# Row runs for v and q, two queues and a new order for the first loads of a fused linear-attention and two-MLP kernel

## The chip, the cores and the metric

The kernel runs on one core of a Trainium2 chip. The metric is the time of one execution on the device, in microseconds. Five engines work side by side, each through its own list of instructions in order: TensorE (PE in the profile; its weight loads are listed as PEld), VectorE (DVE), ScalarE (ACT), GpSimd (POOL) and SyncE (SP). Matmuls write to PSUM, which VectorE and ScalarE read. Transfers between memory (HBM) and the on-chip SBUF are issued by SP, or by ScalarE, and are carried out by 16 DMA engines.

## The reference

```python
# q, k, v: [batch 8, heads 8, sequence 576, head_dim 64]
q_s = exp(q - max(q, axis=-1));  q_s = q_s / (sum(q_s, axis=-1) + 1e-09)
k_s = exp(k - max(k, axis=2));   k_s = k_s / (sum(k_s, axis=2) + 1e-09)
kv = einsum('bhsd,bhse->bhde', k_s, v)
x = einsum('bhsd,bhde->bhse', q_s, kv)       # then to [4608 tokens, 512]
x2 = relu(x @ w_in)**2 @ w_out               # 512 -> 2048 -> 512
g = x2 @ w_gate
out = (silu(g) * (x2 @ w_val)) @ w_out2      # 512 -> 1536 -> 512
```

Softmax runs over head_dim for q and over the sequence for k. The weights come as 64-bit numbers and are turned into 32-bit ones on the chip.

## The kernel before

The 4608 tokens are cut into 9 blocks of 512. The first part of the program goes through the blocks with attention and the first MLP, the second part (from about 720 us on) does the second MLP, with weight operands that the first part has prepared and stored. Products are made as three single-pass matmuls on a high and a low part of each operand (`mm3`, L110; the parts are made by `split`, a cast on ScalarE and a subtraction on VectorE, L104 and L105).

**Attention.** Heads go in four pairs `hp`. `kv_unit(b, hp)` makes the normalised product of k and v for a batch and a pair: maxima over k's rows on VectorE (L336 to L338), a transpose on TensorE and one more maximum (L341, L343), a broadcast back through TensorE (L346), a subtraction (L347), exp on ScalarE (L353), then 12 products of 96 rows, 6 for each head, of k's 64 columns by 65 columns of v (L358). The 65th column of v is ones, so that the last column of the result is the denominator (L363, L364); ScalarE scales the rest (L367). k and v lie in SBUF with 96 partitions of 6 rows of the sequence each: partition p holds rows 6p to 6p + 5. In k these six rows stand in one run; in v each row of 64 is followed by a one, so a load of v lands in runs of 64 numbers (L294). `q_unit` makes q's softmax: a maximum over each row (L376), 8 exps of 64 columns with the maximum as bias, written over the tile (L380), a sum, a reciprocal and a multiplication (L383 to L386). `q_transpose` (L393) and `x_pair` follow, and give the block of x, transposed, as the right operand of the first MLP.

**First MLP.** For each of 16 slices f, `h_mm` makes the first product (`ph<-xT,w`), `g_of` its squared relu, and `acc_mm` adds the second product to four accumulators (`acc<-g,w`). In block 0 the weights are converted on the way: `w1.step(1)` loads a 64-bit tile, takes it to 32 bits in four steps (ScalarE L138, VectorE L140, L144 and L148, through a PSUM buffer of the pool `ps_a`, which has two and also serves `kv_unit` and `q_transpose`), and splits it (ScalarE L189, GpSimd L191). w1 holds `in` and `out` tiles in the order in which the block uses them.

**Order.** The order of SP's instructions is that of the program text (`manual_schedule`). On the other engines it is set when the program is built, by a planner that takes the instructions by their order in the program and by its own estimate of when each could start; on the chip it is fixed. In the head of the program SP loads, by the list in L722, k, q and v of block 0 into space lent by the weight pool, with the first three weight tiles in between; the plan of L735 then starts the units of the four pairs at ticks 0 to 10. Batch 1 and later ones are worked off inside the MLP's slices, as `attention_plan` says.

Of the kernel before, what the change touches and what calls it, by code (L numbers as in the profile page):

```python
# [8 lines left out]
F32 = mybir.dt.float32  # L9
F32R = mybir.dt.float32r  # L10
I32 = mybir.dt.int32
AF = mybir.ActivationFunctionType
ALU = mybir.AluOpType
AX = mybir.AxisListType
# [3 lines left out]
P = 128  # L18
EPS = 1e-9
# [3 lines left out]
def tile_linear_attention_two_mlps(  # L23
# [29 lines left out]
    nc = tc.nc  # L53
    B, H, S, D = q.shape
# [3 lines left out]
    T = 512  # L58
    TJ = T // P
# [5 lines left out]
    CK = 96  # L65
    NC = S // CK
# [5 lines left out]
    const = ctx.enter_context(tc.tile_pool(name="const", bufs=1))  # L72
# [19 lines left out]
    att = ph0.enter_context(tc.tile_pool(name="att", bufs=1, side="right"))  # L92
    sp = ph0.enter_context(tc.tile_pool(name="sp", bufs=2, side="right"))
# [9 lines left out]
    def split(hi, lo, src, eng=None):  # L103
        nc.scalar.copy(hi, src)  # L104
        (eng or nc.vector).tensor_tensor(lo, src, f32(hi), op=ALU.subtract)  # L105
# [172 lines left out]

    kvs = [att.tile([P, NP, 2, P], F32R, name=f"kv{i}") for i in range(2)]
    kf = att.tile([P, P], F32, name="kf")  # L280
    vt1 = att.tile([CK, 2, NC, D + 1], F32, name="vt")
    kts, qs, qT, xT = {}, {}, {}, {}

    def load_k(b, hp, t=None):
# [2 lines left out]
        nc.sync.dma_start(t, k[b, 2 * hp:2 * hp + 2].rearrange("h (p c) d -> p h c d", c=NC))  # L287
        return t

    def load_v(b, hp, t=None):  # L290
        if t is None:
            t = vt1
        for h in range(2):
            nc.sync.dma_start(  # L294
                t[:, h, :, 0:D], v[b, 2 * hp + h].rearrange("(p c) d -> p c d", c=NC)
            )
        return t

    def load_kv(b, hp):
        kt = vt = None  # L300
        if b == 1 and hp % 2:

            kt, vt = (
                raws.tile([P, T], w_in.dtype, name="wraw", tag="wraw").bitcast(F32) for _ in range(2)
            )
            kt = kt[:CK, 0:2 * NC * D].rearrange("p (h c d) -> p h c d", h=2, c=NC)
            vt = vt[:CK, 0:2 * NC * (D + 1)].rearrange("p (h c d) -> p h c d", h=2, c=NC)
            nc.gpsimd.memset(vt[:, :, :, D:D + 1], 1.0)
        kts[b, hp] = load_k(b, hp, kt), load_v(b, hp, vt)

    def runs(i):
# [8 lines left out]
    def load_q(i, hp, t=None):  # L320
        if t is None:
            t = qp.tile([P, TJ, 2, D], F32, name="qs", tag="qs")
        for p0, n, b, s in runs(i):
            for h in range(2):
                nc.sync.dma_start(
                    t[p0:p0 + n, :, h, :],
                    q[b, 2 * hp + h, s:s + n * TJ, :].rearrange("(p j) d -> p j d", j=TJ),
                )
        qs[i, hp] = t

    def kv_unit(b, hp):

        kt, vt = kts.pop((b, hp))
        m3 = sp.tile([CK, 2, NC // 2, D], F32, name="m3", tag="m3", bufs=1)
        m1 = sp.tile([CK, 2, D], F32, name="m1", tag="m1")
        nc.vector.tensor_tensor(m3, kt[:, :, 0:3], kt[:, :, 3:6], op=ALU.max)  # L336
        nc.vector.tensor_tensor(m1, m3[:, :, 0], m3[:, :, 1], op=ALU.max)
        nc.vector.tensor_tensor(m1, m1, m3[:, :, 2], op=ALU.max)  # L338
        yield
        pt = ps_a.tile([P, T], F32, name="pa", tag="pa")  # L340
        nc.tensor.transpose(pt[:, 0:CK], m1.rearrange("p h d -> p (h d)"), ident[:CK, :CK])  # L341
        mx = col.tile([P, 1], F32, name="mx", tag="mx")
        nc.vector.tensor_reduce(mx, pt[:, 0:CK], axis=AX.X, op=ALU.max)  # L343
        yield
        pb = ps_a.tile([P, T], F32, name="pa", tag="pa")
        nc.tensor.transpose(pb[:CK, 0:P], mx.to_broadcast([P, CK]), ident)  # L346
        nc.vector.tensor_tensor(  # L347
            kt, kt,
            pb[:CK, 0:P].rearrange("p (h d) -> p h d", h=2).unsqueeze(2).to_broadcast([CK, 2, NC, D]),
            op=ALU.subtract,  # L350
        )
        yield
        nc.scalar.activation(kt, kt, AF.Exp)  # L353
        yield
        pk = ps_a.tile([P, T], F32, name="pa", tag="pa")
        for c in range(NC):
            for j in range(2):
                nc.tensor.matmul(  # L358
                    pk[j * D:(j + 1) * D, 0:D + 1], lhsT=kt[:, j, c, :], rhs=vt[:, j, c, :],
                    start=(c == 0), stop=(c == NC - 1),  # L360
                )
        rd = col.tile([P, 1], F32, name="rd", tag="rd", bufs=1)
        nc.vector.tensor_scalar(rd, pk[:, D:D + 1], EPS, None, op0=ALU.add)  # L363
        nc.vector.reciprocal(rd, rd)  # L364
        for j in range(2):
            r = slice(j * D, (j + 1) * D)
            nc.scalar.activation(kf[r, r], pk[r, 0:D], AF.Copy, scale=rd[r])  # L367
        kv = kvs[b % 2]
        split(kv[:, hp, 0], kv[:, hp, 1], kf)
        yield  # L370

    def q_unit(i, hp):

        t = qs.pop((i, hp))
        m = sp.tile([P, TJ, 2], F32, name="qm", tag="qm")
        nc.vector.tensor_reduce(m, t, axis=AX.X, op=ALU.max, negate=True)  # L376
        yield
        for j in range(TJ):
            for h in range(2):
                nc.scalar.activation(t[:, j, h], t[:, j, h], AF.Exp, bias=m[:, j, h:h + 1])  # L380
        yield
        r = sp.tile([P, TJ, 2], F32, name="qr", tag="qr")
        nc.vector.tensor_reduce(r, t, axis=AX.X, op=ALU.add)  # L383
        nc.vector.tensor_scalar(r, r, EPS, None, op0=ALU.add)
        nc.vector.reciprocal(r, r)  # L385
        nc.gpsimd.tensor_tensor(t, t, r.unsqueeze(3).to_broadcast([P, TJ, 2, D]), op=ALU.mult)  # L386
        qs[i, hp] = t
# [318 lines left out]


    with tc.manual_schedule(engines={mybir.EngineType.SP}):
        nc.gpsimd.memset(vt1[:, :, :, D:D + 1], 1.0)
        nc.gpsimd.memset(kf, 0.0)  # L710


        def borrowed():
            return f32(w_slot(wpb)).rearrange("p t n -> p (t n)")

        for hp in range(NP):
            kt = borrowed()[:CK, 0:2 * NC * D].rearrange("p (h c d) -> p h c d", h=2, c=NC)
            vt = borrowed()[:CK, 0:2 * NC * (D + 1)].rearrange("p (h c d) -> p h c d", h=2, c=NC)
            nc.gpsimd.memset(vt[:, :, :, D:D + 1], 1.0)
            qt = borrowed()[:, 0:T].rearrange("p (j h d) -> p j h d", h=2, j=TJ)  # L720
            kts[0, hp], qs[0, hp] = (kt, vt), qt
        for what in "k0 k1 q0 v0 k2 q1 k3 v1 w v2 w q2 q3 w v3".split():  # L722
            if what == "w":
                w1.load()
                continue
            hp = int(what[1])
            if what[0] == "k":
                load_k(0, hp, kts[0, hp][0])
            elif what[0] == "v":
                load_v(0, hp, kts[0, hp][1])  # L730
            else:
                load_q(0, hp, qs[0, hp])

        plan = []
        steps = ((1, 1, 5, 8), (1, 2, 5, 9), (2, 3, 7, 10), (4, 4, 8, 10))  # L735
# [14 lines left out]
        for n in range(NB * NF + LAG):  # L750
            i, f = divmod(n, NF)
# [97 lines left out]
```

## Time and profile before

| | |
|---|---|
| median of 3 runs | 1699.56 us (1696.88 to 1700.6) |
| the profiled execution | 1697.3 us |
| its span, first to last instruction | 1695.2 us |
| TensorE busy in it | 1664.2 us, 98% |
| VectorE, ScalarE, GpSimd busy | 930.4, 865.3, 273.8 us |
| mean granted TensorE clock | 0.998 of full speed |

The profile is of one execution, and its times run from the first instruction of its span. A row names the line of the kernel, the engine, the operation, the written tile and the tiles read. Busy shares of TensorE come from modelled ends of pipelined matmuls, so a busy TensorE need not be at its peak.

### The profile page before, as it was taken

Reading aid. Unit: us, or ns where it says so; the run is one execution under the profiler, and the core shown is the slowest. Engines: PE = TensorE matmul, PEld = TensorE weight load, DVE = VectorE, ACT = ScalarE, POOL = GpSimd, SP = SyncE. Lnnn points to the kernel's source line nnn. Section 1 sums busy time; section 2 is a strip of 40 time slices with the busy share of each in tenths; the row PEclk is TensorE's granted clock in tenths of the full one; section 3 lists DMA queues with packets and bytes.
Section 4 is the critical chain, followed back from the end, with each engine's and each line's share of the span. In section 5 each row is a group of like instructions: output and inputs, shape, how many; then the busy total and the mean of one; then the engine's idle time right before and its main releaser. Section 6 shows DMA issues by size and latency. Waiting matters only on the chain.

```text
span 1695.2 us, 23439 instructions
## 1 busy us (share of the span) xinstructions
PE 1664.2 (98%) x8406; PEld 1377.4 (81%) x8406; DVE 930.4 (55%) x1650; ACT 865.3 (51%) x1701; POOL 273.8 (16%) x260
## 2 busy tenths in 40 slices
PE   5999999999999999999999999999999999999998
PEld 3778888878888887788788888888878888888898
DVE  7884545555554564554242457644765476446646
ACT  6885656555565655665443345333543354335434
POOL 2661101112010111111000211021101210121020
PEclk9999999999999999999999999999999999999999
DMA  9653434443443434332233677867686678666897
GB/s 231 177 165 89 128 108 134 144 115 111 128 128 120 144 124 115 108 131 88 81 100 99 191 217 215 248 196 214 212 244 192 205 214 260 197 199 203 252 387 276
DMA packets 221315, 292.00 MB, mean 172 GB/s; under 512 B 124816, under 2 KB 152464, under 8 KB 221200
## 3 DMA queue, kind: packets, MB, share of 16 engines
q1 hardware_dynamic: 220080, 289.33, 55.6%
q8 instruction: 67, 1.10, 0.3%
q10 hardware_dynamic: 1120, 1.18, 0.2%
q14 instruction: 48, 0.39, 0.1%
HBM read 238.55 MB, written 51.90 MB: 171 GB/s over the span
## 4 chain that ended last, share of the span: by engine, by line
PE 91%; DVE 3%; DMA 2%; ACT 2%; issue 1%; POOL 0%; SPq 0%; DVEq 0%; ACTq 0%; POOLq 0%
PE ps L110 45%; PE ph L110 22%; PE acc L110 21%; PE pa L358 1%; PE pa L393 1%; DMA od<-wst 1%; DMA x<-x2d 1%; DVE wst L105 1%; ACT wst L104 0%; ACT w L380 0%; DMA wraw<-in_moe_w_out_dram 0%; DVE wbits L148 0%; DMA kt<-in_k_dram 0%; DVE pa L144 0%; DVE xT L105 0%
## 5 line engine op out<-in xcount | busy, mean ns | idle before, releaser
L110 PE MATMUL ps<-xo,wu 128*128 128x512 f32 (+1 forms) x2520 | 518.2, 368 | 0.0
L110 PEld LDWEIGHTS ps<-xo,wu 128*128 128x128 f32 x2520 | 439.0, 189 | 78.7
L110 PE MATMUL acc<-g,w 128*128 128x512 f32 x1728 | 433.1, 396 | 4.6 <-ACT g L104 1.8
L110 PE MATMUL ph<-xT,w 128*128 128x512 f32 x1728 | 421.4, 393 | 2.3 <-ACT w L189 1.2
L110 PEld LDWEIGHTS ph<-xT,w 128*128 128x128 f32 x1728 | 321.8, 188 | 72.9 <-ACT w L189 1.6
L110 PEld LDWEIGHTS acc<-g,w 128*128 128x128 f32 x1728 | 316.3, 188 | 76.1 <-DVE g L105 4.1
L110 PE MATMUL ps<-uo,wu 128*128 128x512 f32 (+1 forms) x1260 | 259.9, 368 | 1.3 <-DVE uo L105 1.3
L110 PEld LDWEIGHTS ps<-uo,wu 128*128 128x128 f32 x1260 | 219.3, 189 | 41.2 <-DVE uo L105 2.1
L460 ACT ACTIVATE r<-ph 128x512 f32<-128x512 f32 x144 | 86.3, 599 | 220.6 <-PE ph L110 220.2
L105 DVE TENSOR_TENSOR g<-r,g 128x512 fp32r<-128x512 f32 x128 | 91.5, 715 | 190.4 <-ACT g L104 190.4
L104 ACT CAST uo<-u 128x512 fp32r<-128x512 f32 (+1 forms) x210 | 120.8, 580 | 124.7 <-PE ps L110 53.4
L659 POOL TENSOR_TENSOR u<-u 128x512 f32<-128x512 f32 (+1 forms) x30 | 35.4, 1181 | 761.2 <-DVE u L655 761.2
L105 DVE TENSOR_TENSOR uo<-u,uo 128x512 fp32r<-128x512 f32 (+1 forms) x210 | 131.6, 645 | 47.4 <-ACT uo L104 47.3
L654 DVE TENSOR_TENSOR u<-u,ps 128x512 f32<-128x512 f32 (+1 forms) x60 | 38.0, 634 | 215.9 <-ACT u L653 215.9
L609 ACT COPY ps<-ps 128x512 f32<-128x512 f32 x126 | 72.0, 571 | 136.6 <-PE ps L110 135.4
L461 ACT ACTIVATE r<-r 128x512 f32<-128x512 f32 x144 | 91.2, 633 | 3.0
L104 ACT CAST g<-r 128x512 fp32r<-128x512 f32 x144 | 89.4, 621 | 3.2
L235 POOL TENSOR_TENSOR wsum<-wbits 128x256 f32<-128x256 f32 x36 | 35.3, 990 | 308.4 <-DVE wbits L148 255.0
L380 ACT ACTIVATE qs<-qs,qm 128x64 f32<-128x64 f32 x256 | 69.6, 340 | 21.0 <-DVE qm L376 15.5
L386 POOL TENSOR_TENSOR qs<-qs,qr 128x512 f32<-128x512 f32 x32 | 34.4, 1076 | 250.8 <-DVE qr L385 146.5
L653 ACT ACTIVATE u<-ps 128x512 f32<-128x512 f32 (+1 forms) x60 | 33.4, 556 | 51.6 <-PE ps L110 51.5
L618 ACT COPY p<-ps 128x512 f32<-128x512 f32 x63 | 37.1, 588 | 41.6 <-PE ps L110 40.9
(111 smaller groups left out, 1404.5 us busy)
## 6 DMA issues: line engine op xcount, KB each, us to landing
wu<-gvd SPq DMA_DIRECT2D x210, 512.0 KB, 4.4
wu<-od SPq DMA_DIRECT2D x105, 512.0 KB, 4.4
gvd<-wst SPq DMA_DIRECT2D x84, 256.0 KB, 2.3
od<-wst SPq DMA_DIRECT2D x42, 256.0 KB, 2.2
w<-in_moe_w_in_dram SPq DMA_DIRECT2D x16, 512.0 KB, 6.5
w<-in_moe_w_out_dram SPq DMA_DIRECT2D x16, 512.0 KB, 5.2
x2d<-e SPq DMA_DIRECT2D x32, 256.0 KB, 2.4
x<-x2d SPq DMA_DIRECT2D x32, 256.0 KB, 5.4
```

The lines of the kernel that those rows point to most:

```text
L104: nc.scalar.copy(hi, src)
L105: (eng or nc.vector).tensor_tensor(lo, src, f32(hi), op=ALU.subtract)
L110: nc.tensor.matmul(ps, lhsT=w[s], rhs=x[t], start=start and n == 0, stop=stop and n == 2, skip_group_check=more,)
L235: nc.gpsimd.tensor_tensor(to, x, y, op=op)
L380: nc.scalar.activation(t[:, j, h], t[:, j, h], AF.Exp, bias=m[:, j, h:h + 1])
L386: nc.gpsimd.tensor_tensor(t, t, r.unsqueeze(3).to_broadcast([P, TJ, 2, D]), op=ALU.mult)
L460: nc.scalar.activation(r, ph, AF.Relu)
L461: nc.scalar.activation(r, r, AF.Square)
L609: nc.scalar.copy(x, y)
L618: nc.scalar.copy(x, y)
L654: nc.vector.tensor_tensor(u, u, gate, op=ALU.mult)
L659: nc.gpsimd.tensor_tensor(s1, a21, a22, op=ALU.add)
```

## The change

Four things are changed. v's tiles get another layout: three groups for six rows, each with a one, two rows of 64 in a run, and a one (130 numbers); a load lands in runs of 128 numbers. A product with an even row reads the one ahead of its row and writes columns 0 to 64 of the result, one with an odd row reads the one behind its row and writes columns 1 to 65, so that the denominator is the sum of columns 0 and 65. Two products with a column of zeros come first and write column 65. This holds for all 32 units. q of block 0 is loaded by one DMA for a pair, four rows in a run, into a tile of its own; the exps read it and write the tile in the order used before. The first loads are ordered anew: v of pairs 0 and 1 is issued by ScalarE, all else by SP, and the three weight tiles come after the last q. An exp of one column is put in front of them on ScalarE.

```diff
@@ -278,7 +278,8 @@
 
     kvs = [att.tile([P, NP, 2, P], F32R, name=f"kv{i}") for i in range(2)]
     kf = att.tile([P, P], F32, name="kf")
-    vt1 = att.tile([CK, 2, NC, D + 1], F32, name="vt")
+    vt1 = att.tile([CK, 2, NC // 2, 2 * D + 2], F32, name="vt")
+    zero = const.tile([P, 1], F32, name="zero")
     kts, qs, qT, xT = {}, {}, {}, {}
 
     def load_k(b, hp, t=None):
@@ -287,12 +288,22 @@
         nc.sync.dma_start(t, k[b, 2 * hp:2 * hp + 2].rearrange("h (p c) d -> p h c d", c=NC))
         return t
 
-    def load_v(b, hp, t=None):
+    def v_words(words):
+
+        t = words[:CK, 0:NC * (2 * D + 2)].rearrange("p (h m e) -> p h m e", h=2, m=NC // 2)
+        v_ones(t)
+        return t
+
+    def v_ones(t):
+        nc.gpsimd.memset(t[:, :, :, 0:2 * D + 2:2 * D + 1], 1.0)
+
+    def load_v(b, hp, t=None, by=nc.sync):
         if t is None:
             t = vt1
         for h in range(2):
-            nc.sync.dma_start(
-                t[:, h, :, 0:D], v[b, 2 * hp + h].rearrange("(p c) d -> p c d", c=NC)
+            by.dma_start(
+                t[:, h, :, 1:2 * D + 1],
+                v[b, 2 * hp + h].rearrange("(p m x) d -> p m (x d)", m=NC // 2, x=2),
             )
         return t
 
@@ -304,8 +315,7 @@
                 raws.tile([P, T], w_in.dtype, name="wraw", tag="wraw").bitcast(F32) for _ in range(2)
             )
             kt = kt[:CK, 0:2 * NC * D].rearrange("p (h c d) -> p h c d", h=2, c=NC)
-            vt = vt[:CK, 0:2 * NC * (D + 1)].rearrange("p (h c d) -> p h c d", h=2, c=NC)
-            nc.gpsimd.memset(vt[:, :, :, D:D + 1], 1.0)
+            vt = v_words(vt)
         kts[b, hp] = load_k(b, hp, kt), load_v(b, hp, vt)
 
     def runs(i):
@@ -353,18 +363,25 @@
         nc.scalar.activation(kt, kt, AF.Exp)
         yield
         pk = ps_a.tile([P, T], F32, name="pa", tag="pa")
+        for j in range(2):
+            nc.tensor.matmul(
+                pk[j * D:(j + 1) * D, D + 1:D + 2], lhsT=kt[:, j, 0, :], rhs=zero[:CK],
+                start=True, stop=False, skip_group_check=True,
+            )
         for c in range(NC):
+            m, x = divmod(c, 2)
             for j in range(2):
                 nc.tensor.matmul(
-                    pk[j * D:(j + 1) * D, 0:D + 1], lhsT=kt[:, j, c, :], rhs=vt[:, j, c, :],
-                    start=(c == 0), stop=(c == NC - 1),
+                    pk[j * D:(j + 1) * D, x:x + D + 1], lhsT=kt[:, j, c, :],
+                    rhs=vt[:, j, m, x * (D + 1):(x + 1) * (D + 1)],
+                    start=(c == 0), stop=(c == NC - 1), skip_group_check=True,
                 )
         rd = col.tile([P, 1], F32, name="rd", tag="rd", bufs=1)
-        nc.vector.tensor_scalar(rd, pk[:, D:D + 1], EPS, None, op0=ALU.add)
+        nc.vector.tensor_scalar(rd, pk[:, 0:1], pk[:, D + 1:D + 2], EPS, op0=ALU.add, op1=ALU.add)
         nc.vector.reciprocal(rd, rd)
         for j in range(2):
             r = slice(j * D, (j + 1) * D)
-            nc.scalar.activation(kf[r, r], pk[r, 0:D], AF.Copy, scale=rd[r])
+            nc.scalar.activation(kf[r, r], pk[r, 1:D + 1], AF.Copy, scale=rd[r])
         kv = kvs[b % 2]
         split(kv[:, hp, 0], kv[:, hp, 1], kf)
         yield
@@ -373,11 +390,14 @@
 
         t = qs.pop((i, hp))
         m = sp.tile([P, TJ, 2], F32, name="qm", tag="qm")
-        nc.vector.tensor_reduce(m, t, axis=AX.X, op=ALU.max, negate=True)
+        src = t
+        if i == 0:
+            src, t = src[0].rearrange("p h j d -> p j h d"), t[1]
+        nc.vector.tensor_reduce(m, src, axis=AX.X, op=ALU.max, negate=True)
         yield
         for j in range(TJ):
             for h in range(2):
-                nc.scalar.activation(t[:, j, h], t[:, j, h], AF.Exp, bias=m[:, j, h:h + 1])
+                nc.scalar.activation(t[:, j, h], src[:, j, h], AF.Exp, bias=m[:, j, h:h + 1])
         yield
         r = sp.tile([P, TJ, 2], F32, name="qr", tag="qr")
         nc.vector.tensor_reduce(r, t, axis=AX.X, op=ALU.add)
@@ -706,7 +726,8 @@
 
 
     with tc.manual_schedule(engines={mybir.EngineType.SP}):
-        nc.gpsimd.memset(vt1[:, :, :, D:D + 1], 1.0)
+        v_ones(vt1)
+        nc.gpsimd.memset(zero, 0.0)
         nc.gpsimd.memset(kf, 0.0)
 
 
@@ -715,11 +736,18 @@
 
         for hp in range(NP):
             kt = borrowed()[:CK, 0:2 * NC * D].rearrange("p (h c d) -> p h c d", h=2, c=NC)
-            vt = borrowed()[:CK, 0:2 * NC * (D + 1)].rearrange("p (h c d) -> p h c d", h=2, c=NC)
-            nc.gpsimd.memset(vt[:, :, :, D:D + 1], 1.0)
-            qt = borrowed()[:, 0:T].rearrange("p (j h d) -> p j h d", h=2, j=TJ)
+            vt = v_words(borrowed())
+            words = borrowed()
+            qt = (
+                words[:, 0:T].rearrange("p (h j d) -> p h j d", h=2, j=TJ),
+                words[:, T:2 * T].rearrange("p (j h d) -> p j h d", h=2, j=TJ),
+            )
             kts[0, hp], qs[0, hp] = (kt, vt), qt
-        for what in "k0 k1 q0 v0 k2 q1 k3 v1 w v2 w q2 q3 w v3".split():
+        warm = sp.tile([P, TJ, 2], F32, name="qm", tag="qm")
+        nc.scalar.activation(warm[:, 0, 0:1], zero, AF.Exp)
+        load_v(0, 0, kts[0, 0][1], nc.scalar)
+        load_v(0, 1, kts[0, 1][1], nc.scalar)
+        for what in "k0 q0 k1 q1 k2 v2 q2 k3 v3 q3 w w w".split():
             if what == "w":
                 w1.load()
                 continue
@@ -729,7 +757,10 @@
             elif what[0] == "v":
                 load_v(0, hp, kts[0, hp][1])
             else:
-                load_q(0, hp, qs[0, hp])
+                nc.sync.dma_start(
+                    qs[0, hp][0].rearrange("p h j d -> p h (j d)"),
+                    q[0, 2 * hp:2 * hp + 2, 0:T, :].rearrange("h (p j) d -> p h (j d)", j=TJ),
+                )
 
         plan = []
         steps = ((1, 1, 5, 8), (1, 2, 5, 9), (2, 3, 7, 10), (4, 4, 8, 10))
```

## Rows read from the trace of the kernel before

**Rows 1.** The page: busy time, share of the span and instructions of TensorE.
```profile
PE 1664.2 (98%) x8406; PEld 1377.4 (81%) x8406; DVE 930.4 (55%) x1650; ACT 865.3 (51%) x1701; POOL 273.8 (16%) x260
```
**Rows 2.** Stretches: length, busy time of each engine, granted clock, DMA share, GB/s.
```profile
113.00:720.00 607.00, 605.60 (x3265) 494.47 (x3265) 319.87 (x623) 356.78 (x751) 97.56 (x100) 1.00 0.40 122
```
**Rows 3.** Waits of TensorE from 113 to 720 us: total, times, longest.
```profile
PE acc L110 <- POOL g L105: 1.3, 1, 1.3
...
PE pa L346 <- DVE mx L343: 0.4, 1, 0.4
```
**Rows 4.** The chain of waits: start, length, what ran.
```profile
40.26 2.59 PE ph L110 x10
```
**Rows 5.** VectorE in order of time: start, length, operation, [idle before, ended by].
```profile
4.02 0.55 DVE L336 TENSOR_TENSOR m<-w 96x384 f32<-96x384 f32 x1 [4.02 <-DMA w<-in_k_dram]
...
22.92 0.68 DVE L376 TENSOR_REDUCE qm<-w 128x8 f32<-128x512 f32 x1
...
24.70 0.68 DVE L148 SCALAR_TENSOR_TENSOR wbits<-w,pa 128x512 int32<-128x512 int32 x1
...
31.75 0.16 DVE L363 TENSOR_SCALAR rd<-pa 128x1 f32<-128x1 f32 x1 [1.19 <-PE pa L358]
```
**Rows 6.** Two stretches of the head; PE, PEld, DVE, ACT, POOL, clock, DMA, GB/s.
```profile
4.00:20.29 16.29, 8.71 (x65) 6.03 (x66) 12.72 (x35) 11.10 (x29) 2.39 (x2) 1.00 1.19 245
20.29:37.51 17.22, 12.04 (x80) 7.48 (x78) 13.17 (x29) 11.22 (x32) 3.36 (x3) 0.80 0.97 272
```
**Rows 7.** DMA packets from 2 to 12 us, then from 23.5 to 28 us.
```profile
DMA packets 5345, 2.35 MB, mean 235 GB/s; under 512 B 4507, under 2 KB 5345, under 8 KB 5345
...
DMA packets 980, 1.71 MB, mean 381 GB/s; under 512 B 57, under 2 KB 737, under 8 KB 980
```
**Rows 8.** DMA issues of SP in order of time.
```profile
8.40 0.99 SPq L120 DMA_DIRECT2D w<-in_moe_w_in_dram  x1
...
12.39 4.33 SPq L325 DMA_DIRECT2D w<-in_q_dram  x4
...
17.93 1.27 SPq L294 DMA_DIRECT2D w<-in_v_dram  x2
```
**Rows 9.** DMA issues at 8.4 and at 12.4 us: KB, us to landing.
```profile
w<-in_moe_w_in_dram SPq DMA_DIRECT2D x1, 512.0 KB, 6.6
...
w<-in_q_dram SPq DMA_DIRECT2D x1, 128.0 KB, 6.3
```
**Rows 10.** ScalarE in order of time.
```profile
5.56 1.28 ACT L380 ACT_TABLE_LOAD   x1 [5.56 <-DMA w<-in_q_dram]
7.96 2.03 ACT L380 ACTIVATE w<-w,qm 128x64 f32<-128x64 f32 x8 [1.12 <-DVE qm L376]
...
19.55 0.65 ACT L138 ACTIVATE pa<-w 128x512 f32<-128x512 f32 x1
...
21.87 2.03 ACT L380 ACTIVATE w<-w,qm 128x64 f32<-128x64 f32 x8
...
27.57 0.84 ACT L353 ACTIVATE w<-w 96x768 f32<-96x768 f32 x1
```
**Rows 11.** TensorE in order of time.
```profile
25.44 0.45 PE L346 MATMUL pa<-ident,mx 128*96 128x128 f32 x1 [2.57 <-DMA w<-in_moe_w_out_dram]
...
30.21 1.49 PE L358 MATMUL pa<-w 96*64 96x65 f32 x24
```
**Rows 12.** Stretch from 26 to 28 us, columns as in rows 6.
```profile
26.00:28.00 2.00, 0.54 (x3) 0.55 (x4) 1.34 (x4) 1.96 (x7) 1.51 (x2) 0.50 1.06 386
```
**Rows 13.** The chain of waits from 129 to 137.5 us.
```profile
129.48 0.85 PE pa L358 x24
...
133.28 0.95 PE ph L110 x6
...
134.67 0.70 PE acc L110 x3
```
**Rows 14.** The stretch from 113 to 720 us, line L358 alone: TensorE, weight loads.
```profile
113.00:720.00 607.00, 23.01 (x600) 19.55 (x600) 1.00 0.40 122
```

## The prediction

> **What bounds the kernel now.** I read the page first, then the stretches, the waits, the chain of waits, and then the first 40 us instruction by instruction. The page says that TensorE is busy nearly throughout [rows 1]. The stretch from 113 to 720 us, in which seven of the eight batches of k and v are worked off beside the first MLP, shows why that can be trusted there: TensorE has almost no gap [rows 2], and all its waits in 607 us are three pairs with 2.6 us together [rows 3]. In that stretch a matmul more is time more, and a transfer that lands sooner is worth nothing. What loads can be worth lies at the head: the chain of waits reaches the first long run of matmuls (the second product of the first block) only at 40.26 us [rows 4]. So the case has two halves, the head, where something may be gained, and everything behind it, where only TensorE's instructions count.
>
> In the head, look at VectorE. From its first instruction at 4.02 us, which waits for k's first tile [rows 5], to 20.29 us it is busy 12.72 of 16.29 us, and from there to 37.51 us 13.17 of 17.22 us [rows 6]. It is the busiest engine of both, has 3.57 and 4.05 us of gaps, and nothing can bring the head below its work. The transfers run without a pause meanwhile: DMA share about 1 or above in both stretches [rows 6]. They run at very different rates: from 2 to 12 us 5345 packets, 4507 of them under 512 B, moved 2.35 MB, from 23.5 to 28 us 980 packets moved 1.71 MB at 381 GB/s [rows 7]. Taking the 4507 as 256 B (one row of q or v), they are 1.15 MB; if the other 1.20 MB went at 381 GB/s they took 3.1 us, and the short ones had 6.9 us, some 170 GB/s.
>
> Last, who waits for what lands. k's first tile is waited for; hardly anything else is, directly. But q of pairs 2 and 3 is issued from 12.39 us in four DMAs, the first landing 6.3 us later, and v of pair 3 from 17.93 us [rows 8, 9]. So the first of those tiles comes at 18.7 us, and ScalarE makes their exps at 21.87 us and again at 24.27 us, two groups of 8 with 2.03 us each, in front of pair 3's own k exp at 27.57 us [rows 10]. On VectorE the same tiles put two maxima and two sums (0.68 us each, one shown) between the first weight's bit steps, whose last ends at 25.38 us [rows 5]. TensorE's broadcast for pair 3 starts at 25.44 us after 2.57 us of wait; the profile names a weight's DMA, but that had landed long before, and what ended 0.06 us earlier is that bit step, which held one of the two PSUM buffers of this pool [rows 5, 11]. [...]
>
> **The change part by part.**
>
> *Loads of the first block.* v in runs of two rows is 512 B, q in runs of four is 1 KB. q and v of the block are 1024 + 1152 KB, 2.2 MB. At 170 GB/s that is 13 us of transfer; at 381 GB/s it would be 5.8, so up to 7 us less, and nothing less if longer runs don't help. For 512 B no row shows a rate; I take it half way, 275 GB/s, and for 1 KB 360. Then k, q and v (3.4 MB with k) take 3.3 + 2.9 + 4.3 = 10.5 us from 2 us on, and the last q lands at 13 to 14.5 us, where before the first of the late ones came at 18.7. k's first tile stays first on SP and keeps its 4.0 us. k of pair 1 now stands behind q of pair 0 and shares the engines with the v on ScalarE's queue: at 360 GB/s shared by two it lands near 6.3 us, one microsecond later than VectorE took it up. VectorE has the maximum of q in between, so I count 0.5 us lost.
>
> *Weights last.* The first weight tile was issued at 8.40 us and landed 6.6 us later, at 15.0 us [rows 8, 9]; its first use is ScalarE's scaling at 19.55 us, in front of the bit steps, so 4.5 us are spare. Behind 3.4 MB and with its own 0.5 it lands at 2 + 3.9 MB at 360 to 235 GB/s, so 13 to 19 us, still before its use. If q and v kept 170 GB/s the bytes in front would last until about 18 us and it would come at 20, 0.5 us late.
>
> *v of pairs 0 and 1 on ScalarE's queue, exp table first.* One v DMA costs its queue 0.64 us (1.27 for two [rows 8]), four cost 2.6 us, or 4.3 if they were held up as q's four were [rows 8]. Behind the table load (1.28 us [rows 10]) ScalarE is free again at about 5.3 to 7 us; its first exps started at 7.96 us, after a wait for VectorE [rows 10], so this is covered. The table load was covered as well (5.56 to 6.84 us), so moving it gains nothing by itself. [...] The DMA share shows engines that were full with one queue.
>
> *What the head gains.* q's exps of pairs 2 and 3 (4.06 us of ScalarE) and four reductions with their small steps (3.4 us of VectorE) can move ahead of 20.29 us, into VectorE's 3.57 us of gaps. With 0.5 us lost at k and not every gap usable, I take 2 us by 20.29 us. After it pair 3's k exp no longer stands behind 4 us of q exps, the bit step ends earlier, TensorE's pause shrinks and its clock has less cause to fall; of the 4.05 us of gaps I take half, 2 us. So the head gains 4.0 us. Bounds: nothing, if the order in which VectorE and ScalarE work stays as it is, and 7.6 us if every gap goes. Everything behind the head shifts with it, since TensorE is nearly full from 40 us on.
>
> *Two more matmuls in every k-v unit.* The new zero products are 96x64 by 96x1, before the 12 products of each unit. The trace records 24 matmuls for 12 [rows 11], so two more are four, 0.85 us / 24 = 0.035 us each at the full clock [rows 13]: 0.142 us for a unit. Does a column less make them cheaper? Near the same place, three 512-column products take 0.70 us, and the same columns cut into six pieces take 0.95 us [rows 13], 0.083 us for each short piece more, with weights of 128 columns, whatever its columns. So time here goes with instructions and weight loads, not with streamed columns, and I take the full price. The 600 records of the stretch from 113 to 720 us [rows 14] are 25 units: 25 x 0.142 = 3.55 us, with nothing to hide them. Three units of batch 1 fall between 57 and 113 us, where TensorE still has some pauses: 0.15 us of their 0.43. The four of batch 0 lie in the head. Sum 3.7 us. Bounds: 0, if one column costs nothing, and 28 units x 4 x 0.042 (half of 0.083, for half the weight columns) = 4.7 us. [...]
>
> *The rest.* The denominator adds two PSUM columns in one VectorE instruction as before; exps read and write other addresses; the memsets stay as many plus one. Loads of v behind block 0 become shorter in a stretch where nobody waits for them. All nothing; their cover is the full TensorE.
>
> **Sum.** The profiled execution took 1697.3 us (span 1695.2 and 2.1 around it). 1697.3 - 4.0 + 3.7 = 1697.0. The median of the runs is 2.3 us above the profiled one, so 1699.3 us for a median: no change that can be told, within 0.2% (3.4 us, about what a measurement of this kernel can tell from nothing).
>
> **The rivals.**
> 1. *The head packs tightly.* All of VectorE's gaps go: -7.6 + 3.7 = -3.9, 1695.7 us. For it: the transfers were the only unbroken load of the head. Against it: several gaps are round trips between engines (PSUM to ScalarE to VectorE), which data does not shorten. Chance 0.17.
> 2. *The one-column products are nearly free:* -4.0 + 0, 1695.6 us. Against it stands the price of the short pieces. Chance 0.08.
> 3. *Slower: the head gains nothing.* The order on VectorE and ScalarE is fixed when the program is built; if q of pairs 2 and 3 stays behind the first weight's steps there, earlier landing is only earlier waiting, and the 28 units remain: +3.7, 1703.3 us. It decides as soon as the head gains under 0.3 us. For it: hardly a wait for q or v is seen in the head. Chance 0.15.
> 4. *Loads cost what the short pieces cost:* -4.0 + 4.7, 1700.3 us, inside the forecast's own band.
>
> **How the numbers follow.** My forecast, with rival 4 in it, has 0.60 and its own range is 1696 to 1702.9 us. Faster by over 0.2% are rivals 1 and 2, 0.25; slower is rival 3, 0.15. The range takes rivals 1 and 2 with about 1 us of the spread of runs, and ends at rival 3: 1694.5 to 1703.3 us.
>
> **What would show it.** In the profile after: the L358 group's successor has 28 instead of 24 matmuls a unit and some 0.99 us in the chain; q's reductions of pairs 2 and 3 stand before 20 us on VectorE; the first weight's bit steps end before 25 us; the clock falls less between 24 and 31 us; the second product of the first block starts near 36 us instead of 40.26. The prediction is wrong if that start moves by more than 7 us or not at all, or if the chain shows the new products at no cost.

## The result: 1% slower

The changed kernel took 1717.08 us (median of 5 runs, 1716.69 to 1718.83), the kernel before 1700.6 us beside it (1696.88 to 1703.24): a ratio of 1.0099, 95% interval 1.0083 to 1.0116. The forecast was 1699.3 us, no change, with a range to 1703.3. The profiled execution has a span of 1714.9 us against 1695.2, so there are 19.7 us to find in the trace. (Single executions of one kernel differ by several us, as the ranges show, so the trace tells where, and ratios of several runs tell how much.)

Most of it is at a place of which the prediction has no term: the second part of the kernel, behind the first MLP and all attention, which the diff doesn't touch. (Its first product starts at 912.7 us before, not near 720 us as said above, and at 920.0 us after.) It runs the same 3780 matmuls in both kernels, from the first to the last in 777.7 us before and 789.9 us after. The groups of line L110 that make its 512-column products (busy time, the mean ns of one, and the engine's idle time before them), and a stretch of 50 us there, first of the kernel before, then after:

```profile
L110 PE MATMUL ps<-xo,wu 128*128 128x512 f32 x2016 | 457.6, 389 | 0.0
```
```profile
1100.00:1150.00 50.00, 50.00 (x222) 41.40 (x221) 21.00 (x32) 17.59 (x30) 11.60 (x9) 1.00 0.66 196
```
```profile
L110 PE MATMUL ps<-xo,wu 128*128 128x512 f32 x2016 | 469.7, 395 | 0.0
```
```profile
1100.00:1150.00 50.00, 50.00 (x217) 40.31 (x216) 21.61 (x33) 16.66 (x28) 7.76 (x6) 1.00 0.68 202
```

TensorE waits for nothing in either and its clock is 1.00 in both; it only does 217 matmuls where it did 222. 2016 x 6 ns = 12.1 us. From the page, TensorE in all [rows 1]: 128 instructions more, but 20.7 us more of busy time.

```profile
PE 1684.9 (98%) x8534; PEld 1383.0 (81%) x8534; DVE 952.5 (56%) x1650; ACT 865.1 (50%) x1702; POOL 274.2 (16%) x261
```

The new products cost a little less than forecast. The chain of waits in block 1, to set beside [rows 13]:

```profile
131.38 2.73 PE ph L110 x12
134.11 0.21 PE pa L367 x4
134.32 0.75 PE pa L374 x24
```

0.96 us a unit against 0.85, so 0.11 us more where 0.142 was forecast. Third, the head: the chain there, to set beside [rows 4].

```profile
41.80 1.29 POOL w L191
43.09 0.04 issue
43.13 4.08 PE ph L110 x10
```

The second product of block 0 starts 2.9 us later, not 4 us earlier, and takes 4.08 us instead of 2.59, at a mean granted clock of 0.59 from 43.13 to 47.21 us (before, 1.00 from 40.26 to 42.85). VectorE in order of time [rows 5], then SyncE's issues [rows 8], and what the SyncE queue waited for from 0 to 30 us (total, times, longest):

```profile
4.03 0.56 DVE L346 TENSOR_TENSOR m<-w 96x384 f32<-96x384 f32 x1 [4.03 <-DMA w<-in_k_dram]
...
7.58 0.56 DVE L346 TENSOR_TENSOR m<-w 96x384 f32<-96x384 f32 x1 [1.87 <-DMA w<-in_k_dram]
...
9.24 0.69 DVE L396 TENSOR_REDUCE qm<-w 128x8 f32<-128x512 f32 x1 [0.74 <-DMA w<-in_q_dram]
...
11.47 0.56 DVE L346 TENSOR_TENSOR m<-w 96x384 f32<-96x384 f32 x1 [0.58 <-DMA w<-in_k_dram]
...
17.35 0.69 DVE L396 TENSOR_REDUCE qm<-w 128x8 f32<-128x512 f32 x1
...
27.33 0.68 DVE L148 SCALAR_TENSOR_TENSOR wbits<-w,pa 128x512 int32<-128x512 int32 x1
```
```profile
4.03 0.31 SPq L288 DMA_DIRECT2D w<-in_k_dram  x1
8.43 1.65 SPq L304 DMA_DIRECT2D w<-in_v_dram  x2
```
```profile
SPq L304 <- DMA w<-in_v_dram: 4.3, 2, 4.0
```

k of pair 1 lands at 7.48 us and VectorE waits 1.87 us for it; SyncE issues nothing from 4.3 to 8.4 us, because its next load waits for the completion of a v load that ScalarE had issued (landed at 8.35 us): the program as built gives its loads eight completion semaphores in turn, over both queues, and this load's was still that v's. The head's stretches, columns as in [rows 6], and the DMA packets from 2 to 12 us [rows 7]:

```profile
4.00:20.29 16.29, 5.71 (x63) 4.21 (x63) 12.61 (x34) 10.58 (x35) 2.51 (x3) 1.00 0.98 263
20.29:37.51 17.22, 14.59 (x91) 9.80 (x92) 10.08 (x25) 9.57 (x24) 2.95 (x3) 1.00 0.82 255
40.00:45.00 5.00, 3.18 (x10) 1.92 (x11) 4.82 (x8) 3.88 (x7) 2.75 (x3) 0.88 0.33 105
45.00:50.00 5.00, 5.00 (x19) 4.00 (x18) 2.04 (x4) 2.73 (x5) 2.37 (x2) 0.78 0.36 105
```
```profile
DMA packets 3036, 2.33 MB, mean 233 GB/s; under 512 B 176, under 2 KB 3036, under 8 KB 3036
```

VectorE's gaps before 20.29 us are 3.68 us, as before (3.57), with waits for loads in them that weren't there. The packets are longer (176 under 512 B instead of 4507), the rate is the same, SyncE's pause included.

Together: 12.2 us in the second part; 4.2 us by the third product of block 0, which starts at 49.88 us instead of 45.67; and 0.11 us in each of some 25 units, 2.7 us. That is 19.1 of the 19.7 us.

### The profile page after: what moved, and what is told of

Its sections match the earlier page's. It is cut to its first block, busy times and chain, and to the rows that moved or that the text cites. A ratio compares the mean times of both kernels' runs of the same rounds, so it can differ in the third digit from the quotient of the medians.

```text
span 1714.9 us, 23648 instructions
## 1 busy us (share of the span) xinstructions
PE 1684.9 (98%) x8534; PEld 1383.0 (81%) x8534; DVE 952.5 (56%) x1650; ACT 865.1 (50%) x1702; POOL 274.2 (16%) x261
## 4 chain that ended last, share of the span: by engine, by line
PE 92%; DVE 3%; DMA 2%; ACT 2%; issue 1%; SPq 0%; POOL 0%; DVEq 0%; ACTq 0%; POOLq 0%
PE ps L110 45%; PE ph L110 22%; PE acc L110 22%; PE pa L374 1%; DMA x<-x2d 1%; PE pa L413 1%; DMA w<-in_k_dram 1%; DVE wbits L148 0%; PE pa L367 0%; DMA wraw<-in_moe_w_out_dram 0%; ACT pa L138 0%; DVE xo L105 0%; DVE g L105 0%; DMA qs<-in_q_dram 0%; DVE pa L144 0%
## 5 line engine op out<-in xcount | busy, mean ns | idle before, releaser
L110 PE MATMUL ps<-xo,wu 128*128 128x512 f32 (+1 forms) x2520 | 529.8, 372 | 0.0
L110 PEld LDWEIGHTS ps<-xo,wu 128*128 128x128 f32 x2520 | 438.6, 188 | 90.6
L110 PE MATMUL acc<-g,w 128*128 128x512 f32 x1728 | 433.8, 396 | 3.0 <-DVE g L105 1.9
L110 PE MATMUL ph<-xT,w 128*128 128x512 f32 x1728 | 424.2, 394 | 3.3 <-ACT w L189 2.1
L110 PEld LDWEIGHTS ph<-xT,w 128*128 128x128 f32 x1728 | 322.8, 189 | 75.3 <-ACT w L189 2.8
L110 PEld LDWEIGHTS acc<-g,w 128*128 128x128 f32 x1728 | 316.6, 188 | 75.2 <-DVE g L105 5.2
L110 PE MATMUL ps<-uo,wu 128*128 128x512 f32 (+1 forms) x1260 | 261.7, 369 | 0.2 <-DVE uo L105 0.2
L110 PEld LDWEIGHTS ps<-uo,wu 128*128 128x128 f32 x1260 | 219.1, 188 | 42.0 <-DVE uo L105 0.7
L105 DVE TENSOR_TENSOR g<-r,g 128x512 fp32r<-128x512 f32 x128 | 98.3, 768 | 177.6 <-ACT g L104 175.8
```

The lines of the kernel that those rows point to most:

```text
L110: nc.tensor.matmul(ps, lhsT=w[s], rhs=x[t], start=start and n == 0, stop=stop and n == 2, skip_group_check=more,)
```

## The experiments

### Where the big tiles stand

What does the change do to the second part? The tile `zero`, one column, takes 32 bytes a partition on the left side of SBUF, in front of the big tiles there. By the addresses that the programs were built with, the left-hand tiles of the second part (6 of 9 `wu`, 14 of 28 `xo`, `uo`) stood at 640 beyond multiples of 2048 before and at 672 after; the right-hand ones (3 `wu`, 14 `xo`) stay at 1920. Theory: where they stand sets the pace. Rival: something else of the change lasts into the second part.

**e1**, the changed kernel with a tile of 64 bytes.

```diff
-    zero = const.tile([P, 1], F32, name="zero")
+    zero = const.tile([P, 16], F32, name="zero")[:, 0:1]
```

> The changed kernel with one difference: the tile of zeros takes 64 bytes of each partition instead of 32, so that every tile laid out behind it starts at a multiple of 64 bytes again, as in the kernel before. Theory A (the second MLP is slower because the 32-byte tile moves the tiles of one side of SBUF, and not of the other, to 32 past a multiple of 64): a 512-column matmul of the second part takes 226.7 ns again instead of 232.7, the part is 12.2 us shorter, about 1705 us. Rival B (the pace comes from something else that the change brings, such as other transfers): it stays at 1717.

1716.28 us, ratio 1.0098 (1.0083 to 1.0113), second part 790.2 us: another 32 bytes change nothing. A start at a multiple of 64 isn't what counts, so theory A falls in this form; the time is what rival B had, and e2 tells whether B holds.

**e2**, the kernel before and 32 bytes that nothing reads.

```diff
     make_identity(nc, ident)
+    pad = const.tile([P, 1], F32, name="pad")
+    nc.gpsimd.memset(pad, 0.0)
```

> The kernel before, and nothing of the change but a 32-byte tile in the same place, set once and never read. Theory A: the second part takes 12 us more, about 1712.8 us, and the head is as before. Rival B: 1700.6, as before.

1712.05 us, ratio 1.0075 (1.0060 to 1.0090), second part 789.6 us. An unused tile does it alone, and the rival falls. **e3** has the same tile on the right side too (`padr`, from a pool with `side="right"`), so that the sides stand at 672 and 1888.

> The kernel before with a 32-byte tile on each side of SBUF, so that all large tiles start 32 past a multiple of 64. Theory A1 (what costs is that weights and moving operand lie at different places modulo 64): no cost, 1700.6. Theory A2 (what costs is a start that is no multiple of 64): 12 us or more, 1712.8 or above, and the first MLP slower too.

1713.52 us, ratio 1.0084 (1.0067 to 1.0101), second part 789.9 us: A1 falls, and the time is what A2 had, but the first MLP, whose operands all stand on the left, isn't slower (394 and 396 ns a product over the run, 393 and 396 before). Is it the distance, then, or the address itself? **g1** is the kernel before with 128 bytes at the right edge for the second part alone; **g2** is e2 with 224 bytes there (`[P, 56]`), which makes the distance between the sides a multiple of 256 again while all tiles stand at 32 beyond multiples of 64.

```diff
                         ph0.close()
+                        gap = ctx.enter_context(tc.tile_pool(name="gap", bufs=1, side="right"))
+                        nc.gpsimd.memset(gap.tile([P, 32], F32, name="gap"), 0.0)
```

> The kernel before with 128 bytes, set once and never read, between the right edge of SBUF and the right-hand tiles of the second part, which then stand 128 bytes lower; the left-hand ones stay. Theory (what counts is how far a product's weights and its moving operand stand apart, and only what is left after whole steps of 128 bytes): the second part stays at 777.8 us and the time at about 1700 us. Rival (the step is 256 bytes or more): the products that take one operand from each side slow down as in e1, the second part takes 785 to 790 us and the time is 1707 to 1712 us.

> The kernel before with the 32 bytes of e2 on the left and 224 bytes on the right for the second part: every big tile of the second part then stands at 32 beyond a multiple of 64, on both sides alike. Theory (the distance of weights and moving operand counts, not where they stand): the second part is back at 777.8 us, and the time is about 1700 us (1700 to 1702, since the first part keeps the 32 bytes on the left alone). Rival (a tile that doesn't begin at a multiple of 64 is slower by itself): 790 us for the second part, and about 1712 us.

g1: 1705.95 us, ratio 1.0043 (1.0025 to 1.0061), a little under the rival's range. g2: 1699.05 us, ratio 0.9997 (0.9986 to 1.0009). The group of rows above, in e2, g1 and g2 (line numbers shift with the edits):

```profile
L112 PE MATMUL ps<-xo,wu 128*128 128x512 f32 x2016 | 469.7, 395 | 0.0
```
```profile
L110 PE MATMUL ps<-xo,wu 128*128 128x512 f32 x2016 | 464.8, 392 | 0.0
```
```profile
L112 PE MATMUL ps<-xo,wu 128*128 128x512 f32 x2016 | 457.6, 389 | 0.0
```

| | left, right (beyond 2048) | distance modulo 256 | mean of one, ns | second part, us |
|---|---|---|---|---|
| before | 640, 1920 | 0 | 389 | 777.7 |
| g2 | 672, 1696 | 0 | 389 | 777.8 |
| g1 | 640, 1792 | 128 | 392 | 784.6 |
| e1, e3 | 704, 1920; 672, 1888 | 192 | 395 | 790.2, 789.9 |
| after, e2 | 672, 1920 | 224 | 395 | 789.9, 789.6 |

g2 settles it: the addresses of after on the left, the pace of before. So A2 falls too: what counts in these runs is how far the two sides stand apart. g1 refutes the step of 128 that I expected; 256 fits all rows. In the trace of before one product of the group starts every 226.7 ns and lasts 389, so they overlap.

The trace of after, set beside the addresses of the program as built, narrows it down. Of the part's 512-column products, those with one operand on each side start every 233.8 ns. Those with both on one side, but an operand of the product before or of the two behind on the other, start every 231.1 ns, and those with all of these on one side every 226.9 ns, as in the kernel before. So in after the products that start later are those whose operands, or those of neighbouring products, stand on both sides. Other engines and transfers don't account for it: of the products with `xo`, which start every 232.7 ns, the 232 beside which VectorE, ScalarE and GpSimd did next to nothing start every 232.5, and the 163 with the DMA engines under 5% busy every 232.7. What in TensorE takes the time is not shown.

**f1** takes it out of the change: the zero column shares the tile of `rd`, which is as large as it was.

```diff
-    zero = const.tile([P, 1], F32, name="zero")
+    rdz = col.tile([P, 8], F32, name="rd", tag="rd", bufs=1)
+    rd, zero = rdz[:, 0:1], rdz[:, 1:2]
...
-        rd = col.tile([P, 1], F32, name="rd", tag="rd", bufs=1)
```

> The changed kernel with one thing different: the zero column and the reciprocal's column share one tile of the small pool, as large as the reciprocal's tile was, so that no big tile on the left of SBUF is moved from where it stood before the change. Theory (where the big tiles stand sets the pace of the second part's 512-column products): the second part, from its first to its last product, is back at about 777.8 us instead of 789.9, and the time is about 1717 - 12 = 1705 us. Rival (the second part is slower for another cause, such as what the changed first part leaves behind): it stays at 790 us and the time at about 1717 us.

1705.82 us, ratio 1.0037 (1.0022 to 1.0052); mean of one again 389 ns. The second part takes 780.0 us; in it TensorE waits 3.0 us for VectorE's `uo`, 1.3 before.

### The zero products, the queue and the order of the loads

**f2** is f1 without the zero products (the loop with `rhs=zero[:CK]` deleted).

> f1 without the two products by the zero column at the head of each unit's sums; nothing else is left out. Theory (they cost what the chain of waits shows, 0.10 us in each of 25 units): about 2.5 to 2.9 us less than f1, 1702 us. Rival from the prediction (0.142 us a unit): 3.6 us less. Rival (one-column products lie beside others): no difference to f1.

1702.34 us, ratio 1.0017 (1.0008 to 1.0026): 0.0020 under f1, 3.4 us, near the forecast's 3.7. (The intervals are too wide to tell it from the 2.5 to 2.9 us of the chain.) The unit is back at the length of [rows 13]:

```profile
132.78 0.85 PE pa L370 x24
```

The other kernels change the line with the loads. With all on SyncE the two calls with `nc.scalar` are deleted. h2 has four such calls.

```diff
 after, f2  v0, v1 by ScalarE         "k0 q0 k1 q1 k2 v2 q2 k3 v3 q3 w w w"
+f3, h1     (SyncE alone)             "k0 q0 k1 q1 v0 v1 k2 v2 q2 k3 v3 q3 w w w"
+e4, f4     (SyncE alone)             "k0 k1 q0 v0 k2 q1 k3 v1 v2 q2 q3 v3 w w w"
+g3         (SyncE alone)             "k0 k1 q0 v0 k2 q1 k3 v1 w v2 w q2 q3 w v3"
+g4         v0, v1 by ScalarE         "k0 k1 q0 k2 q1 k3 v2 q2 q3 v3 w w w"
+h2         v0 to v3 by ScalarE       "k0 k1 q0 k2 q1 k3 q2 q3 w w w"
```

e4 is e1 with its line; f3 is f1 with its line; the others have no zero products and the tiles of f1.

> The changed kernel with the 64-byte tile of zeros, and the first loads all on SP, in the order of the kernel before but with the three weight tiles behind them. Theory C (the head lost its 4.3 us because v of pairs 0 and 1, issued beside, delays k of pair 1 and holds up SP): the second product of the first block starts at 40 us or earlier instead of 43.1, total 1705 less 3 to 5, 1700 to 1702. Rival D (the new order on VectorE and ScalarE costs it, whichever queue is used): 1705, as with both queues.

> f1 with v of pairs 0 and 1 issued by SyncE again, behind q of pair 1, so that all first loads are on one queue in otherwise the new order. Theory (the second queue is what costs at the head: its v runs share the engines with k of pair 1, and SyncE waits for their semaphore until 8.4 us): the second product of block 0 starts near 41 us instead of 43.1, and the time is about 3 us under f1, 1702 us. Rival (the order costs, weights last and q ahead of k, not the queue): within 1 us of f1, 1705 us.

> f1 without the two zero products a unit and with the first loads on SyncE alone in the order of before, the weights behind them: what is left of the change is the runs of two rows of v and of four rows of q, weights last, and the table loaded in front. Theory (the new layout of v and q gains little, since the path to block 0's second product goes on through k and the weights): f1 less 2.9 for the zero products and 3 for the queue and order, about 1699 us, within 1.5 us of before. Rival from the prediction (the loads that land sooner shorten the head by 4 us): 1695 us.

> f4 with the weights loaded at their old places among q and v, so that the order of the loads is that of before; what is left of the change is the runs of two and four rows and the table loaded in front. Theory (the wider runs are worth nothing, the weights' place little): within 1.5 us of f4's 1699 us. Rival (weights last held the head up, as block 0's second product waits for the weights): 1 to 3 us less, 1696 to 1698 us, and the second product of block 0 starts before 40 us.

> f2 (no zero products, rd tile shared) with the two v of pairs 0 and 1 still issued by ScalarE, but the other loads in the order of before: k of pair 1 ahead of q of pair 0, k of pairs 2 and 3 ahead of v and q. Beside f2 (1702.3) and f4 (1699.0) it takes queue and order apart. Theory (the second queue costs): as f2, about 1702 us, and SyncE still waits until 8.4 us for the semaphore that the first v holds. Rival (the order of q ahead of k costs): as f4, about 1699 us.

> f3 without the two zero products a unit: one queue, q ahead of k and the weights last, so that beside f4 only the order among k, q and v differs. Theory (the second queue is what costs at the head): as f4, about 1699 us. Rival (q ahead of k costs, whatever the queue): as f2, 1702 us, with the second product of block 0 a microsecond or more behind f4's 41.1 us.

> g4 with all four pairs' v of block 0 issued by ScalarE, eight loads on its queue ahead of its work, and k and q alone on SyncE in the order of before. Theory (loads on the second queue cost by sharing the transfers with k, and by the semaphores that SyncE then waits for): k of pair 2 or 3 lands later than in g4, and the time is 1702 to 1705 us. Rival (the second queue costs nothing and g4's 1702 us has another cause): 1699 to 1700 us, since v then lands earlier than anywhere else.

| | us | ratio to before | interval | 2nd product at, us |
|---|---|---|---|---|
| e4 | 1713.60 | 1.0085 | 1.0070 to 1.0100 | 39.98 (e1: 43.10) |
| f3 | 1704.00 | 1.0026 | 1.0014 to 1.0039 | 43.42 |
| f2, queue and order | 1702.34 | 1.0017 | 1.0008 to 1.0026 | 41.78 |
| g4, queue | 1702.05 | 1.0017 | 1.0007 to 1.0026 | 40.60 |
| h1, order | 1701.56 | 1.0018 | 1.0006 to 1.0030 | 41.06 |
| h2, queue twice | 1704.47 | 1.0027 | 1.0017 to 1.0037 | 43.88 |
| f4, neither | 1698.97 | 0.9998 | 0.9986 to 1.0011 | 41.12 |
| g3, order of before | 1698.30 | 0.9994 | 0.9984 to 1.0004 | 40.84 |

Queue and order together cost 0.0019, about 3 us (f2 to f4). f4, g3, g4 and h2 came out as their theories had it. e4 did so for the second product, not for the time, since its 64 bytes take nothing back. f3 and h1 went against theirs, and f3 has the later second product and the shorter time beside f1 (42.54 us, 1705.82 us): where that product starts in one execution doesn't tell the time. More of the queue costs more by the medians, and h2 shows how: SyncE's waits to 30 us, its issues, and what VectorE waited for up to 45 us.

```profile
SPq L289 <- DMA w<-in_v_dram: 4.5, 2, 4.3
```
```profile
1.67 0.45 SPq L757 DMA_DIRECT2D w<-in_q_dram  x1
6.46 0.32 SPq L289 DMA_DIRECT2D w<-in_k_dram  x1
```
```profile
DVE m L347 <- DMA w<-in_k_dram: 7.6, 2, 4.0
```

After two k and one q SyncE stands for 4.3 us, until a v of the other queue has landed; k of pair 2 goes out at 6.46 us (3.55 in f4) and VectorE waits 3.6 us for it. But g4 and h1 are not settled: each has a median some 3 us above f4, and neither's profiled execution shows a later second product (g4's is its fastest, 1698.68 us). By the ratios each alone costs about what both cost together, with intervals that touch f4's; how, these traces don't show.

### Why early loads are worth nothing

f4 has the wide runs, one queue and all of k, q and v landed by 16.3 us (before: 23.6), and gains nothing. Its packets from 2 to 12 us, its stretches of the head, and ScalarE's exps of k:

```profile
DMA packets 3190, 2.58 MB, mean 258 GB/s; under 512 B 189, under 2 KB 3190, under 8 KB 3190
```
```profile
4.00:20.29 16.29, 7.35 (x63) 5.25 (x63) 13.31 (x38) 11.41 (x40) 3.31 (x3) 1.00 1.13 290
20.29:37.51 17.22, 14.03 (x81) 8.68 (x79) 11.17 (x24) 9.63 (x22) 2.32 (x2) 1.00 0.73 230
40.00:45.00 5.00, 4.38 (x12) 3.14 (x12) 3.83 (x6) 2.50 (x5) 3.59 (x3) 0.67 0.39 135
```
```profile
14.29 0.84 ACT L364 ACTIVATE w<-w 96x768 f32<-96x768 f32 x1 [0.92 <-DVE w L358]
...
30.02 0.84 ACT L364 ACTIVATE w<-w 96x768 f32<-96x768 f32 x1
```

VectorE does only 0.6 us more before 20.29 us, and its gaps behind that grow to 6.05 us. Pair 3's k landed at 10.8 us; its exp runs at 30.02 us. The head is built from numbered steps, and pair 3's unit starts in step 4, so on each engine it stands behind the first weight's work. **i1** starts it in step 2, **i3** does that in the kernel before, **i2** packs all steps closer.

```diff
-        steps = ((1, 1, 5, 8), (1, 2, 5, 9), (2, 3, 7, 10), (4, 4, 8, 10))
+i1, i3  steps = ((1, 1, 5, 8), (1, 2, 5, 9), (2, 3, 7, 10), (2, 4, 8, 10))
+i2      steps = ((1, 1, 4, 7), (1, 2, 4, 8), (2, 2, 6, 9), (2, 3, 7, 9))   # range(10)
```

> f4 with one number of the head's plan changed: the k-v unit of pair 3 starts in step 2 instead of step 4, beside pair 2's. In f4 pair 3's k landed at 10.8 us and its exp ran at 30.0 us. Theory (the fixed order of the head's steps is what keeps loads that land early from being worth anything): pair 3's sums come before 27 us instead of 31.7, block 0's second product starts near 38 to 39.5 us instead of 41.1, and the time is 1696 to 1698 us. Rival (the second product waits for the weights' conversion, wherever pair 3 stands): it starts at 41 us again, and the time is about 1699 us.

> i1 with the plan packed further: the transposes and the products by q a step earlier, q of pairs 2 and 3 a step earlier, and ten steps instead of eleven. Theory (the plan's order): another 0.5 to 1.5 us less than i1. Rival (the engines' work, not the plan, fills the head): as i1, or slower, since ScalarE and VectorE then stand in a queue in front of the first weight.

> The kernel before with the same one number changed as in i1, and nothing of the change. Its v of pair 3 lands at 23.6 us. Theory: pair 3's sums can't start before v has landed, but its k work moves ahead of the weight; 0 to 1.5 us less than before, 1698 to 1699.5 us, and less gain than i1. Rival (k's work of pair 3 in front of the first weight holds the weight up): up to 2 us more, 1701 us.

i1: 1699.08 us, ratio 1.0000 (0.9987 to 1.0013). i2: 1699.36 us, 1.0005 (0.9996 to 1.0013). i3: 1700.58 us, 1.0009 (1.0000 to 1.0018). i2 and i3 came out as their rivals had it, with the second product at 40.06 and 41.44 us. TensorE in i1:

```profile
38.36 2.58 PE L110 MATMUL ph<-xT,w 128*128 128x512 f32 x10 [0.17 <-POOL w L191]
42.13 0.96 PE L110 MATMUL acc<-g,w 128*128 128x512 f32 x3 [1.19 <-ACT w L189]
43.49 2.34 PE L110 MATMUL acc<-g,w 128*128 128x512 f32 x9 [0.40 <-POOL w L191]
45.67 2.88 PE L110 MATMUL ph<-xT,w 128*128 128x512 f32 x12
```

The order was what held the second product: it starts at 38.36 us, as expected, 2.8 us earlier than in f4. But the next weight isn't converted (L189, L191), TensorE waits 1.19 and 0.40 us for it, and the third product starts at 45.67 us, to the hundredth where it started before the change. The 1.9 us gained on the kernel before are given back there, and the time doesn't move. Both theories were half right: first the plan holds the head, then the weights' conversion. One thing stays open: in f4's profiled execution the third product starts at 47.86 us, 2.2 us later than in i1, and the medians are still the same.

## Why the prediction was wrong, step by step

- **"The rest ... All nothing"** is the step that failed most. It counted the new tile's memset, not its 32 bytes. They cost 0.0062 of the time, 10.5 us (after to f1), and 12.2 us in the trace. The words "where only TensorE's instructions count" took the price of an instruction for fixed; it went from 389 to 395 ns in 2016 of them.
- **"What the head gains", 4.0 us**: nothing is gained even where the loads land early (f4, 0.9998). The bound "nothing, if the order in which VectorE and ScalarE work stays as it is" names the cause, and so does rival 3, but at another place: q of pairs 2 and 3 did move ahead of the first weight's steps, and what stayed behind is pair 3's k (f4's exp at 30.02 us). That rival 3's "head gains nothing" came out is in part luck. Gaps of VectorE were no measure: those that f4 fills early come back as 6.05 us later.
- **"Loads of the first block"**: 275 and 360 GB/s were taken for the longer runs. From 2 to 12 us f4 moved 258 GB/s and g3, with the order of before, 267, against 235 before; after moved 233, with SyncE's pause in it. None of f2, f3, f4, g3, g4, h1 and h2 came over 272 (h2), so longer packets were worth much less than the sum took.
- **"k of pair 1 ... 0.5 us lost", "so this is covered"**: k of pair 1 landed at 7.48 us instead of 6.3. After k's first tile VectorE waits 1.87 + 0.74 + 0.58 us for loads before 12 us, and SyncE 4.0 us for a v of the other queue. So ScalarE's idle time didn't cover its loads of v here. Two queues moved no more bytes at once (f2 255 GB/s with two, f4 258 with one), as the reading of engines full with one queue had it; left out is that SyncE waited for loads of ScalarE's queue, 4.0 us in after and 4.3 in h2. Queue and order together cost 3 us.
- **"Two more matmuls", +3.7**: right within what these runs can tell. 0.11 us a unit in the trace, 3.4 us by ratios.
- **The signs**: q's reductions of pairs 2 and 3 did move ahead of 20 us but for pair 3's sum (21.2 us); the first weight's last bit step ends at 28.0 us, not before 25; the second product starts at 43.13 us, not near 36. The clock from 24 to 31 us did rise, from 0.55 to 1.00, but the fall came later: 0.60 from 43 to 47.2 us, where it was 1.00. TensorE was busy 6.12 of the 7 us from 24 to 31 (before 3.99); that its shorter pause kept the clock up was the author's estimate, and no run shows it. Rival 3, at 1703.3 us, was the nearest case; with nothing gained and 3 us lost it is f1's 1705.8 us, and the tiles' places make the rest.

## What to carry to other kernels

Ask of each new tile what it moves: compare the addresses of the operands of the longest loop before and after, and put small tiles where they fill space already taken (f1: 389 ns a product again instead of 395). Before valuing a load that lands earlier, find the first instruction that uses it and see whether it waits for the load or for its place in the engine's order. A second queue made the first wait 4.0 us here (after) and moved no more bytes (255 GB/s in f2, 258 in f4): watch the first queue's own waits.

## What was not expected of the hardware

- In these runs the mean time of a product in the second part's largest group went with the distance of the two sides' tiles modulo 256 bytes: 389 ns at 0 (before, g2), 392 at 128 (g1), 395 at 192 (e1, e3) and at 224 (after, e2). It shows as no wait (0.0 us before the group in after) and no fall of the clock (1.00 from 1100 to 1150 us). Only these four distances were tried.
- Behind the same short waits the granted clock was lower for some microseconds in some runs (0.59 from 43.13 to 47.21 us in after, 0.50 from 114.4 to 116.4 us in e2) and stayed at 1.00 in others (from 40.26 to 42.85 us in the kernel before). The second product of block 0 has the same waits in front of it in the kernel before and in f4 (0.23, 1.19 and then 0.6 us):

```profile
40.26 2.58 PE L110 MATMUL ph<-xT,w 128*128 128x512 f32 x10 [0.63 <-POOL w L191]
```
```profile
41.12 4.13 PE L110 MATMUL ph<-xT,w 128*128 128x512 f32 x10 [0.62 <-POOL w L191]
```

  It takes 4.1 us in after too, 3.85 (f3) to 4.15 us (f1, i3) in f1, f2, f3, g3, g4, h1, h2 and i3, and 2.58 us in i1 (behind 0.17 us of wait) and 2.54 in i2, near the kernel before's 2.58; in e2 the clock is 1.00 from 20 to 60 us. Later ten products stand behind the same wait in the kernel before and in e2, each with a stretch of its own (in e2 a wait of 0.73 us had ended 2.1 us earlier, in the kernel before there was none):

```profile
113.02 2.57 PE L110 MATMUL acc<-g,w 128*128 128x512 f32 x10 [1.35 <-POOL g L105]
```
```profile
113.00:115.00 2.00, 1.98 (x9) 1.64 (x10) 1.97 (x4) 1.80 (x5) 2.00 (x2) 1.00 0.85 292
```
```profile
114.40 4.04 PE L112 MATMUL acc<-g,w 128*128 128x512 f32 x10 [1.34 <-POOL g L107]
```
```profile
114.40:116.40 2.00, 2.00 (x5) 1.61 (x6) 1.90 (x4) 1.81 (x4) 2.00 (x2) 0.50 0.86 322
```

  With the lower clock the ten products take 1.55 us more in the first two rows and 1.47 in the last two. What decides it stays open.
